# Decode attention and gated MLP on one core: VectorE work moved to ScalarE, one weight chunk loaded by rows, and a small product repeated while TensorE waits

## The chip, the cores and the metric

The kernel runs on one core of a Trainium2 chip. The metric is the device time of one execution in microseconds; lower is better. A separate profiled execution gives the trace.

## The reference

One decode step of a transformer layer in float32, for eight sequences with one new token each. The model width is 1024; there are 32 query heads over 4 key and value heads of size 128, a window of the last 1024 cached positions, and an MLP of width 3584.

```python
x = A_x                                       # (8, 1, 1024)
def attention(x):
    q = (x @ wq).reshape(8, 1, 32, 128)       # wq 1024 x 4096
    k, v = the last 1024 positions of the caches, each shared by 8 query heads
    p = softmax(q @ k.T * 128 ** -0.5)
    return (p @ v).reshape(8, 1, 4096) @ wo   # wo 4096 x 1024
def mlp(x):
    return (gelu(x @ w_gate) * (x @ w_up)) @ w_down   # 1024 x 3584, twice; 3584 x 1024
h = x + attention(layernorm(x))
out = h + mlp(layernorm(h))
```

Every weight and every cache entry is used once for eight tokens, so some 111 MB have to come in from HBM for little arithmetic.

## The kernel before

**Loads.** SyncE (SP) issues all weight loads, in order, into two SBUF buffers `buf[0]` and `buf[1]` of 64 KB a partition (8.4 MB). There are seven passes `k`: the query projection, scores, values, the output projection (`WO`), two for gate and up (`GU0`, `GU1`) and one for the down projection (`DN`). Each has a half `a` on `buf[0]` and a half `b` on `buf[1]`; the last has `a` only. A load waits until TensorE has finished with its buffer. Behind those come the late loads: three parts `wd0` to `wd2` of the last `a` half (steps 0 to 3, 4 to 6 and 7, by `CUTS`), three `singles` `ws0` to `ws2` (one 128-row chunk of the down matrix each, 512 KB, 4 KB a row), and the last chunk in two column blocks `we0` and `we1` (`ends`, 256 KB each). Last come 15 tiny `tag` loads; the k-th longest of them has k rows.

**TensorE** runs one loop over the passes (L457). In each half it first turns a token tile (`turn`, L441: eight 128x128 transposes into the PSUM tile `tt`), then makes `products` (L450): eight steps of four matmuls, which stand abreast in four column groups of 32; each float32 matmul is two records in the trace. Steps 0 to 3 go into the first half of the accumulator `ob[s]`, steps 4 to 7 into the second. TensorE waits at L434 on a counter `go`, which GpSimd raises: GpSimd walks the waits of all passes in TensorE's order (L422 to L429). In pass `WO` there are two more products: `fold` (L469), which brings the attention output into the order of the rows, and `res` (L475), which brings the residual `h_sb` into the output's order in `fin`.

**Between the halves** VectorE and ScalarE turn a finished accumulator into the next tokens: scaling, softmax, the value sum over the eight sequences that share a tile (one instruction each, L302 and L305), GELU times up, and copies from `tt` into the token tiles `st` (L242, L270, L288, L312), into `at` (L377), and `widen` (L351). SP and DMA are not waited for there unless a load is late.

**The end.** `d1` gathers the last accumulator's two halves and `d0` (residual and early parts): L396 after step 3 and L398 after step 7. Then `add` (L485) makes, for each of `ws0` to `ws2`, eight matmuls into `fin`, with eight for `d1` behind the first of them; L496 does the last chunk, column block by column block. ScalarE copies the two blocks out (L402); SP and ScalarE store them.

**Order and waits.** `Flow` adds a semaphore wait in front of an instruction only where that engine hasn't seen that count yet (`missing`, L55). It does not know what another engine's count implies.

Of the kernel before, what the change touches and what calls it, by code (L numbers as in the profile page):

```python
# [8 lines left out]
P = 128  # L9
B = 8  # L10
# [22 lines left out]
SINGLE = 3  # L33
TAGS = 15


class Flow:


    def __init__(self, nc):  # L40
        self.nc = nc
        self.sems = []
        self.done = {}
        self.seen = {}
        self.own = {}
        for name in ("tensor", "vector", "scalar", "gpsimd"):
            self.own[name] = self.sem(name)
            self.done[name] = 0
# [5 lines left out]

    def missing(self, engine, waits):  # L55
# [4 lines left out]
        for s, v in need.values():  # L60
            self.seen[engine, s.name] = v
        return list(need.values())

# [9 lines left out]
    def run(self, engine, make, *waits, mark=True):  # L73
        ins = self.start(engine, make, waits)
        if not mark:
            return None
        self.done[engine] += 1
        ins.then_inc(self.own[engine], 1)
        return self.own[engine], self.done[engine]

    def move(self, name, out, src, *waits, engine="sync"):
        s = self.sem(name)
        self.start(engine, lambda e: e.dma_start(out, src), waits).then_inc(s, 16)
        return s, 16
# [7 lines left out]
def pe_marks():  # L92

    names = ["t"]
    for k in range(PASSES):
        names += [f"a{k}h", f"a{k}"]
        if k < DN:
            names += [f"ta{k}", f"b{k}h", f"b{k}"]
            if k == WO:
                names += ["fold", "res"]  # L100
            names += [f"tb{k}"]
    return names


def pe_waits():

    names = ["t"]
    for k in range(PASSES):
        names += [f"a{k}", f"a{k}m", f"a{k}l"]
        if k < DN:  # L110
            names += [f"ta{k}", f"b{k}", f"b{k}m"]
            if k == WO:
                names += ["fold", "res"]
            names += [f"tb{k}"]
    return names


def decode_block(nc, x, w, dn, single, ends, outs):
# [3 lines left out]
    names = pe_marks()  # L122
# [12 lines left out]
    xs = [sb(f"xs{i}", P, D) for i in range(2)]  # L135
# [28 lines left out]
    for i in range(SINGLE):  # L164
        t = buf[1][:, i * D:(i + 1) * D]
        singles.append((t, move(f"ws{i}", t, single[i], pe(f"b{GU1}"))))
# [9 lines left out]
    for k in range(TAGS, 0, -1):  # L176
# [8 lines left out]
    h_sb = sb("h_sb", P, D)  # L185
    d0 = sb("d0", P, N)
    clear = [run("gpsimd", lambda e, t=t: e.memset(t, 0.0)) for t in (xs[1], xs[0], h_sb, d0)]
# [6 lines left out]
    to_rows = sb("to_rows", P, 2, ROWS)  # L194
    z = run("gpsimd", lambda e: e.memset(to_rows, 0.0))
# [3 lines left out]
        ident[:, 2 * 32:4 * 32].rearrange("p (c m) -> p c m", c=2)[:, :, 0:B]), z)  # L199
# [11 lines left out]
    need = {}  # L211
# [27 lines left out]
    def tokens_in(ready):  # L239

        xt = t8[:, :, 0:ROWS].rearrange("p n (b s) -> p n b s", s=STEP)[:, :, :, 0]
        a = run("vector", lambda e: e.tensor_copy(  # L242
            st[0].rearrange("p (c r b) -> p c r b", c=NC, b=B),
            xt.unsqueeze(2).to_broadcast([P, NC, P // B, B])), *ready)
        b = run("scalar", lambda e: e.copy(st[1], st[0]), a)  # L245
        return a, b

    ready = layernorm(x_sb, xs[1], x_in, "ln1", clear[0])
# [7 lines left out]
    for s, h in enumerate("ab"):  # L256
        need[f"{h}0"] = [*landed[0, s], *st_ok[s], *o_free[s]]
        half = run("scalar", lambda e: e.mul(tq[s], ob[s][:, 0:N], scale), pe(f"{h}0h"))  # L258
        tok = run("vector", lambda e: e.scalar_tensor_tensor(  # L259
            xs[s][:, 0:N], ob[s][:, N:2 * N], scale, tq[s], op0=ALU.mult, op1=ALU.add),  # L260
            pe(f"{h}0"), half, clear[1 - s])
        o_free[s] = (tok,)
        need[f"t{h}0"] = [tok, *tt_free]
        z = run("vector", lambda e: e.memset(st[s], 0.0), pe(f"{h}0"))
        for k0 in range(2):
            for g in range(2):
                dst = view(st[s], k0 * HB * P + g * 2 * 32, (32, 2), (P + REP, HB), (REP // 2, 2), (1, REP // 2))
                src = view(tt, g * 2 * 32, (HB, 2), (1, HB), (32, 2), (P, REP // 2))
                st_ok[s] = tt_free = (
                    run("vector", lambda e: e.tensor_copy(dst, src), pe(f"t{h}0"), z),)  # L270
# [3 lines left out]
    for s, h in enumerate("ab"):  # L274
        need[f"{h}1"] = [*landed[1, s], *st_ok[s], *o_free[s]]
        nmax, tot, rtot, sh = (
            sb(f"{n}{s}", P, k) for n, k in (("nmax", 1), ("tot", 1), ("rtot", 1), ("share", HB))
        )
        tok = run("vector", lambda e: e.tensor_reduce(  # L279
            out=nmax, in_=ob[s], axis=AX.X, op=ALU.max, negate=True), pe(f"{h}1"))  # L280
# [4 lines left out]
        tok = run("vector", lambda e: e.reciprocal(rtot, tot), tok)  # L285
        share.append((sh, run("vector", lambda e: e.tensor_scalar(
            sh, own, rtot, None, op0=ALU.mult), tok, own_ok)))
        a = run("vector", lambda e: e.tensor_copy(st[s][:, 0:N], tt[:, 0:N]), pe(f"t{h}1"))  # L288
        b = run("scalar", lambda e: e.copy(st[s][:, N:2 * N], tt[:, N:2 * N]), pe(f"t{h}1"))
        st_ok[s] = tt_free = (a, b)  # L290


    for s, h in enumerate("ab"):
        need[f"{h}2"] = [*landed[2, s], *st_ok[s], *o_free[s]]
        sh, tok = share[s]
        out = xs[s][:, 0:DH]
        for i in range(2):
            o3 = ob[s][:, i * N:(i + 1) * N].rearrange("p (b d) -> p b d", b=HB)
            ready = pe(f"{h}2" + "h" * (1 - i))
            for b in range(HB):  # L300
                if (i, b) == (0, 0):
                    tok = run("vector", lambda e: e.tensor_scalar(  # L302
                        out, o3[:, b], sh[:, b:b + 1], None, op0=ALU.mult), tok, ready)
                else:
                    tok = run("vector", lambda e: e.scalar_tensor_tensor(  # L305
                        out, o3[:, b], sh[:, b:b + 1], out, op0=ALU.mult, op1=ALU.add), tok, ready)
# [3 lines left out]
        for g in range(2):  # L310
            turned = tt[:, 64 * g:64 * g + 64].rearrange("p (b h) -> p h b", h=REP)
            tok = run("vector", lambda e: e.tensor_copy(  # L312
# [6 lines left out]
    for s, h in enumerate("ab"):  # L319
# [12 lines left out]
        h_sb[0:ROWS], x_sb, fin[0:ROWS]), pe("fold"), clear[2])  # L332
    need["res"] = [h_ok]
    run("scalar", lambda e: e.copy(d0[0:32], fin[0:32, 0:N]), pe("res"), clear[3])  # L334
# [9 lines left out]
    ex = sb("ex", 32, N)  # L344
# [3 lines left out]
    def widen(i0, i1, *ready):  # L348

        src = at[:, EARLY + 2 * i0:EARLY + 2 * i1].rearrange("p (i e) m -> p i (e m)", e=2)  # L350
        return run("vector", lambda e: e.tensor_copy(  # L351
# [3 lines left out]
    for k, nb, q0 in ((GU0, NQ, 0), (GU1, DF // N - NQ, NQ * (N // P))):  # L355
# [10 lines left out]
        if k == GU1:  # L366

            first_ok = widen(0, STEPS // 2, pe(f"a{k}"))
            ex_ok = run("scalar", lambda e: e.copy(d0[96:P], g0[96:P]), g_ok, clear[3])
        a = run("vector", lambda e: e.tensor_mul(u0, ge, ob[1][:, 0:N]), pe(f"b{k}h"), ge_ok)  # L370
        b = run("vector", lambda e: e.tensor_mul(u1, ge, ob[1][:, N:2 * N]), pe(f"b{k}"), ge_ok)  # L371
        o_free[1] = (b,)
        hm_ok = run("vector", lambda e: e.tensor_add(xs[1][:, 0:N], u0, u1), a, b, pe(f"tb{k - 1}"))
        need[f"tb{k}"] = [hm_ok, *tt_free]
        if k == GU0:
            used = (run("vector", lambda e: e.memset(ge[96:P], 1.0), b),)
        at_ok = run("vector", lambda e: e.tensor_copy(  # L377
# [4 lines left out]
        if k == GU0:  # L382
            st_ok = [(run("vector", lambda e, s=s: e.tensor_copy(lent[s], at[:, 0:STEPS]), at_ok),)
                     for s in range(2)]
        else:
            late_ok = widen(STEPS // 2, STEPS, at_ok)
            tok = run("scalar", lambda e: e.copy(ex, xs[1][96:P, 0:N]), hm_ok)
            d0_ok = run("vector", lambda e: e.tensor_add(d0[0:32], d0[0:32], ex), tok, res_ok)
    need[f"a{GU1}m"] = landed[GU1, 0][1:]
# [6 lines left out]
    tok = run("vector", lambda e: e.tensor_add(d1, ob[0][:, 0:N], d0), pe(f"a{DN}h"), d0_ok, ex_ok)  # L396
    fl.done["tensor"] = len(names)
    d1_ok = run("vector", lambda e: e.tensor_add(d1, ob[0][:, N:2 * N], d1), pe(f"a{DN}"), tok)  # L398
# [3 lines left out]
    done = [run("scalar", lambda e: e.copy(o_fin[:, a:b], d_ps), (fl.own["tensor"], len(names) + 1 + i))  # L402
# [19 lines left out]
    for name in pe_waits():  # L422
        left = fl.missing("gpsimd", need.pop(name, []))
# [6 lines left out]
    assert not need, need  # L430
# [12 lines left out]

    def products(s, cuts):
        for i in range(STEPS):
            if i in cuts:
# [117 lines left out]
```

## Time and profile before

| | |
|---|---|
| median of 3 runs | 267.03 us (265.92 to 267.09) |
| the profiled execution | 266.8 us, its span 265.5 us |
| TensorE matmuls, busy | 143.2 us (54%), 1024 records |
| VectorE, busy | 39.9 us (15%), 84 instructions |
| ScalarE, busy | 18.3 us (7%), 27 instructions |
| GpSimd, busy | 5.6 us (2%), 15 instructions |
| mean granted TensorE clock | 0.814 |
| moved by DMA | 111.38 MB, mean 420 GB/s |

A row of the page's fifth part, of the groups by line or of a timeline names the kernel's line, the engine, the operation, the tile written and the tiles read. A window row holds the stretch, its length, the busy microseconds and instruction counts of PE, PEld, DVE, ACT and POOL, the granted TensorE clock, the share of the 16 DMA engines that moved data, and GB/s. "DMA to landing" is the time from the issue of a load to its completion.

### The profile page before, as it was taken

To read this page: it belongs to the slowest core of one execution; us is meant where nothing else is said; L and a number is where in the kernel's file an instruction comes from. 1 tells how busy PE (TensorE), PEld (TensorE's weight loads), DVE (VectorE), ACT (ScalarE), POOL (GpSimd) and SP (SyncE) were. 2 spreads that over 40 slices of the span, in tenths; PEclk is the share of its full clock that TensorE was granted. 3 is DMA by queue.
4 is the path that set the end of the run, shared out by engine and by line. 5 is a ranking of instruction groups with operands and counts; after the bars stand their busy time and mean duration, and the time that the engine had idled before them with its cause. 6 is when DMAs were issued, how large, how long until landed. Compare 5 with 4: busy or idle time off the path is not lost. (4 is left out here: it accounts for less than half of the span.)

```text
span 265.5 us, 2397 instructions
## 1 busy us (share of the span) xinstructions
PE 143.2 (54%) x1024; PEld 49.8 (19%) x1024; DVE 39.9 (15%) x84; ACT 18.3 (7%) x27; POOL 5.6 (2%) x15
## 2 busy tenths in 40 slices
PE   0023914915926716717718609717929557527666
PEld 0021211211221112202212202103313212102223
DVE  0330030030030110410410100251001401102301
ACT  1010000200020010000000000031200001000000
POOL 8000000000000000000000000000000000000000
PEclk9999985885865975975986956985898997977959
DMA  8997999899989998999899999999999999999992
GB/s 318 469 454 346 464 474 444 355 464 474 434 365 464 474 425 375 464 474 415 385 464 474 405 395 464 465 395 415 454 405 405 464 400 464 400 459 411 412 406 85
DMA packets 3716, 111.38 MB, mean 420 GB/s; under 512 B 632, under 2 KB 888, under 8 KB 1536
## 3 DMA queue, kind: packets, MB, share of 16 engines
q1 hardware_dynamic: 3552, 111.23, 97.5%
q10 hardware_dynamic: 160, 0.10, 0.1%
q8 instruction: 2, 0.03, 0.0%
q14 instruction: 2, 0.02, 0.0%
HBM read 111.19 MB, written 0.13 MB: 419 GB/s over the span
## 5 line engine op out<-in xcount | busy, mean ns | idle before, releaser
L450 PE MATMUL o<-w,st 128*32 128x512 f32 x832 | 121.5, 746 | 83.7 <-PEq L434 83.7
L450 PEld LDWEIGHTS o<-w,st 128*32 128x32 f32 x832 | 33.7, 133 | 163.0 <-issue 163.0
L441 PE MATMUL tt<-ident,xs 128*128 128x128 f32 x104 | 16.6, 311 | 33.6 <-PEq L434 33.6
L441 PEld LDWEIGHTS tt<-ident,xs 128*128 128x128 f32 x104 | 13.3, 160 | 44.2 <-issue 44.2
L327 DVE TENSOR_TENSOR y_sb<-o,y_sb 128x512 f32<-128x512 f32 x3 | 2.1, 691 | 32.7 <-PE o L450 32.7
L279 DVE TENSOR_REDUCE nmax<-o 128x1 f32<-128x1024 f32 x2 | 2.5, 1225 | 30.1 <-PE o L450 30.1
L259 DVE SCALAR_TENSOR_TENSOR xs<-o,tq 128x512 f32<-128x512 f32 x2 | 1.4, 691 | 32.5 <-PE o L450 32.5
L305 DVE SCALAR_TENSOR_TENSOR xs<-o,share,xs 128x128 f32<-128x128 f32 x14 | 4.9, 350 | 4.3 <-PE o L450 3.8
L281 ACT ACTIVATE xs<-o,nmax 128x1024 f32<-128x1024 f32 x2 | 2.2, 1114 | 37.0 <-DVE nmax L279 37.0
L362 DVE TENSOR_TENSOR g<-o,g 128x512 f32<-128x512 f32 x2 | 1.4, 692 | 22.4 <-PE o L450 22.4
L302 DVE TENSOR_SCALAR xs<-o,share 128x128 f32<-128x128 f32 x2 | 0.7, 351 | 24.4 <-PE o L450 24.4
L325 ACT COPY y_sb<-o 128x512 f32<-128x512 f32 x1 | 0.6, 586 | 50.3 <-PE o L450 50.3
L370 DVE TENSOR_TENSOR u<-ge,o 128x512 f32<-128x512 f32 x2 | 1.4, 688 | 17.6 <-PE o L450 17.6
L371 DVE TENSOR_TENSOR u<-ge,o 128x512 f32<-128x512 f32 x2 | 1.4, 687 | 14.3 <-PE o L450 14.3
L258 ACT ACTIVATE tq<-o 128x512 f32<-128x512 f32 x2 | 1.2, 597 | 30.0 <-PE o L450 30.0
L242 DVE COPY st<-tt 128x1024 f32<-128x1024 f32 x2 | 2.4, 1224 | 4.3 <-PE tt L441 4.3
L361 ACT COPY g<-o 128x512 f32<-128x512 f32 x2 | 1.2, 586 | 26.6 <-PE o L450 26.6
L312 DVE COPY st<-tt 128x512 f32<-128x512 f32 x4 | 2.6, 685 | 2.6 <-PE tt L441 2.6
L245 ACT COPY st<-st 128x1024 f32<-128x1024 f32 x2 | 2.1, 1044 | 10.2 <-DVE st L242 10.2
L226 ACT ACT_TABLE_LOAD x2 | 2.6, 1283 | 2.9 <-POOL ident L182 2.9
L219 DVE BATCH_NORM_STATS2 ln_bn<-x_sb 64x6 f32<-64x512 f32 x2 | 1.3, 677 | 8.3 <-DMA x_sb<-x 8.3
L334 ACT COPY d<-fin 32x512 f32<-32x512 f32 x1 | 0.6, 575 | 28.3 <-PE fin L475 28.3
(59 smaller groups left out, 41.2 us busy)
## 6 DMA issues: line engine op xcount, KB each, us to landing
w<-ends SPq DMA_DIRECT2D x5, 4096.0 KB, 23.6
w<-ends SPq DMA_DIRECT2D x1, 3072.0 KB, 30.5
w<-ends SPq DMA_DIRECT2D x3, 512.0 KB, 15.2
w<-ends SPq DMA_DIRECT2D x1, 1024.0 KB, 32.6
w<-ends SPq DMA_DIRECT2D x2, 256.0 KB, 16.2
w<-w SPq DMA_DIRECT2D x10, 29.2
out<-o_fin SPq DMA_DIRECT2D x1, 64.0 KB, 1.6
out<-o_fin ACTq DMA_DIRECT2D x1, 64.0 KB, 1.7
```

Of the source, the lines that this page charges most:

```text
L226: tok = run("scalar", lambda e: e.activation(sd, ve, AF.Sqrt), tok)
L242: a = run("vector", lambda e: e.tensor_copy(st[0].rearrange("p (c r b) -> p c r b", c=NC, b=B), xt.unsqueeze(2).to_broadcast([P, NC, P // ...
L245: b = run("scalar", lambda e: e.copy(st[1], st[0]), a)
L259: tok = run("vector", lambda e: e.scalar_tensor_tensor(xs[s][:, 0:N], ob[s][:, N:2 * N], scale, tq[s], op0=ALU.mult, op1=ALU.add), pe(f"{h ...
L279: tok = run("vector", lambda e: e.tensor_reduce(out=nmax, in_=ob[s], axis=AX.X, op=ALU.max, negate=True), pe(f"{h}1"))
L281: tok = run("scalar", lambda e: e.activation(xs[s], ob[s], AF.Exp, bias=nmax, accum_out=tot), tok)
L305: tok = run("vector", lambda e: e.scalar_tensor_tensor(out, o3[:, b], sh[:, b:b + 1], out, op0=ALU.mult, op1=ALU.add), tok, ready)
L312: tok = run("vector", lambda e: e.tensor_copy(heads[:, g], turned.unsqueeze(2).to_broadcast([P, REP, P // 2 // B, B])), pe(f"t{h}2"))
L327: tok = run("vector", lambda e: e.tensor_add(y_sb, part, y_sb), ready, tok)
L362: g_ok = run("vector", lambda e: e.tensor_add(g0, ob[0][:, N:2 * N], g0), pe(f"a{k}"), tok)
L441: ins = nc.tensor.transpose(t8[:, i, :], src[:, i * P:(i + 1) * P], ident)
L450: ins = nc.tensor.matmul(ob[s][32 * r:32 * r + 32, c:c + N], st[s][:, i * P + 32 * r:i * P + 32 * r + 32], buf[s][:, (i * NQ + r) * N:(i * ...
```

## The change

1. **VectorE to ScalarE.** The copies out of `tt` (token tiles, score tiles, turned heads, `at`, `lent`, `widen`) become ScalarE copies. The value sum's eight instructions a half become two multiplications over a whole half accumulator and one reduction. Gate times up is summed before it is multiplied. `d0` gets the early part of the down product as a further block of rows instead of an addition. By count 40 VectorE instructions fewer.
2. **GpSimd.** Five memsets of five tiles become one over a tile `zeros` that holds them all.
3. **Waits.** `Flow` keeps with every completion what its engine had waited for (`told`, `implied`), and leaves out a wait that another wait implies. The two lists of TensorE's marks and waits become one list `pe_order`.
4. **`ws0` by rows.** The first single chunk is loaded by three loads, of rows 0 to 31, 32 to 119 (88 rows, by 11 DMA engines) and 120 to 127. Its product leaves `add`: two matmuls of 512 columns, behind step 7, add it into the second half of the last accumulator, so that L398 waits for them.
5. **The repeated product.** TensorE repeats the first matmul of `res` in three gaps: twice in front of step 0 and twice in front of step 4 of the last pass, and four times in front of step 4 of the `b` half of `GU1`. The result lies in `fin` and is overwritten when `ws1` starts its group there.

```diff
+ROWCUTS = (0, 32, 120, P)
+AGAIN = (((0, DN, 2), (STEPS // 2, DN, 2)), ((STEPS // 2, GU1, 4),))
...
+        if i == 0:
+            here = fl.sem("ws0")
+            for a, b in zip(ROWCUTS, ROWCUTS[1:]):
+                fl.start("sync", lambda e: e.dma_start(t[a:b], single[i][a:b]), [pe(f"b{GU1}")]).then_inc(
+                    here, 16)
...
-    clear = [run("gpsimd", lambda e, t=t: e.memset(t, 0.0)) for t in (xs[1], xs[0], h_sb, d0)]
+    clear = run("gpsimd", lambda e: e.memset(zeros, 0.0))
...
-        a = run("vector", lambda e: e.tensor_copy(
+        a = run("scalar", lambda e: e.copy(
             st[0].rearrange("p (c r b) -> p c r b", c=NC, b=B),
...
-            for b in range(HB):
-                if (i, b) == (0, 0):
-                    tok = run("vector", lambda e: e.tensor_scalar(
-                        out, o3[:, b], sh[:, b:b + 1], None, op0=ALU.mult), tok, ready)
-                else:
-                    tok = run("vector", lambda e: e.scalar_tensor_tensor(
-                        out, o3[:, b], sh[:, b:b + 1], out, op0=ALU.mult, op1=ALU.add), tok, ready)
+            tok = run("vector", lambda e: e.scalar_tensor_tensor(
+                av[:, i], o3, rtot, own.unsqueeze(2).to_broadcast([P, HB, DH]),
+                op0=ALU.mult, op1=ALU.mult), tok, own_ok, pe(f"{h}2" + "h" * (1 - i)))
+        tok = run("vector", lambda e: e.tensor_reduce(
+            out=out, in_=av.rearrange("p i b d -> p d (i b)"), axis=AX.X, op=ALU.add), tok)
...
-            d0_ok = run("vector", lambda e: e.tensor_add(d0[0:32], d0[0:32], ex), tok, res_ok)
+            d0_ok = run("scalar", lambda e: e.copy(d0[32:64], xs[1][96:P, 0:N]), hm_ok)
...
-    d1_ok = run("vector", lambda e: e.tensor_add(d1, ob[0][:, N:2 * N], d1), pe(f"a{DN}"), tok)
+    odd_done = fl.own["tensor"], len(names) + 1
+    d1_ok = run("vector", lambda e: e.tensor_add(d1, ob[0][:, N:2 * N], d1), odd_done, tok)
...
+    def repeat_residual(n):
+        with nc.Fori(0, n, engines=[mybir.EngineType.PE]):
+            nc.tensor.matmul(
+                fin[0:32, 0:N], spread.rearrange("p r b -> p (r b)"), h_sb[:, 0:N],
+                start=True, stop=True)
...
     def products(s, cuts):
         for i in range(STEPS):
+            for at_step, k, n in AGAIN[s]:
+                if i == at_step:
+                    with nc.tensor.If(it == k):
+                        repeat_residual(n)
             if i in cuts:
                 wait()
...
-    for i, (t, here) in enumerate(singles):
-        add(lambda j: at[:, LAST - SINGLE + i, :], lambda j: t[:, j * QW:(j + 1) * QW], here,
-            *([res_ok, at_ok] if i == 0 else []), start=(i == 0))
+    (t, here), *rest = singles
+    for ch in range(2):
+        tok = run("tensor", lambda e: e.matmul(
+            ob[0][64 * ch:64 * ch + 32, N:2 * N], at[:, LAST - SINGLE, :], t[:, ch * N:(ch + 1) * N],
+            start=False, stop=True, skip_group_check=True), here, at_ok, mark=(ch == 1))
+    for i, (t, here) in enumerate(rest):
+        add(lambda j: at[:, LAST - SINGLE + 1 + i, :], lambda j: t[:, j * QW:(j + 1) * QW], here,
+            start=(i == 0))
```

More of the change, by code (lines that the diff above doesn't have):

```diff
@@ L121, in decode_block, with before_mark @@
     scale = DH ** -0.5
-    names = pe_marks()
+    order = pe_order()
+    names = [n for kind, n in order if kind == "mark"]
+    need = {}
+    def before_mark(v):
+        out, left = [], v
+        for kind, n in order:
+            if kind == "wait":
+                out += need.get(n, [])
+            else:
+                left -= 1
+                if left == 0:
+                    break
+        return out
+    fl.before_mark = before_mark
     def pe(name):
```

130 lines of the change are left out of this document (69 added, 61 removed).

## The prediction

> **What bounds the kernel now.** I read the page's slices and queues first, then the chain that ended last, then the last 40 us by timeline, loads and narrow windows.
>
> ```profile
> span 265.5 us, 2397 instructions
> ...
> PE 143.2 (54%) x1024; PEld 49.8 (19%) x1024; DVE 39.9 (15%) x84; ACT 18.3 (7%) x27; POOL 5.6 (2%) x15
> ...
> PEclk9999985885865975975986956985898997977959
> DMA  8997999899989998999899999999999999999992
> ...
> q1 hardware_dynamic: 3552, 111.23, 97.5%
> q8 instruction: 2, 0.03, 0.0%
> q14 instruction: 2, 0.02, 0.0%
> ...
> w<-w SPq DMA_DIRECT2D x10, 29.2
> ```
>
> The loads fill the 16 DMA engines for 97.5% of the span; only the last slice is empty. A whole buffer takes 29.2 us from issue to landing, while its 8.4 MB of the 111.23 MB are worth about 19.5 us of the engines (8.4/111.23 of 97.5% of 265.5). So each load is issued some 9.7 us before its turn: what happens between the loads may become microseconds longer without an engine running dry. What can be won lies at the end.
>
> ```profile
> 254.25 6.39 PE o L450 x32
> ...
> 260.73 0.69 DVE d L398
> ...
> 261.48 1.52 PE fin L485 x48
> 263.00 0.26 PE fin L496 x8
> ...
> 263.28 0.48 ACT o_fin L402 x2
> ```
>
> That is the chain: steps 4 to 7 of the last pass, the second sum into d1, 64 small products (two records for each of 32 matmuls), the copies. Beside it stand the loads (first the three of the last pass, wd0 to wd2, then the three single chunks ws0 to ws2, then the end blocks we0 and we1), and how many DMA engines still work:
>
> ```profile
> L83 SPq DMA_DIRECT2D w<-ends x3: 327/432/433, 223.2 to 224.0; - x3
> DMA to landing us min/median/max: 23.6/30.5/32.6
> L83 SPq DMA_DIRECT2D w<-ends x3: 327/432/434, 243.6 to 244.4; - x3
> DMA to landing us min/median/max: 14.3/15.2/16.0
> L83 SPq DMA_DIRECT2D w<-ends x2: 431/434/437, 244.9 to 245.4; - x2
> DMA to landing us min/median/max: 16.1/16.2/16.3
> ```
> ```profile
> 259.60:259.80 0.20, 0.20 (x5) 0.00 (x0) 0.00 (x0) 0.00 (x0) 0.00 (x0) 0.61 0.74 187
> 260.00:260.40 0.40, 0.40 (x8) 0.12 (x4) 0.00 (x0) 0.00 (x0) 0.00 (x0) 1.00 0.23 79
> 260.40:261.00 0.60, 0.60 (x20) 0.35 (x12) 0.27 (x1) 0.00 (x0) 0.00 (x0) 1.00 0.15 50
> 261.00:261.20 0.20, 0.04 (x4) 0.00 (x0) 0.20 (x1) 0.00 (x0) 0.00 (x0) 1.00 0.13 26
> ```
>
> Issue plus time to landing: wd1 lands at about 254.1 (223.6 + 30.5; PE begins step 4 right behind it), wd2 at 256.6, the single chunks at 257.9, 259.1 and 260.4, the end blocks at 261.0 and 261.7. The last column but one, the DMA share, times 16: 11.8 engines work at 259.7, 3.7 at 260.2, 2.4 at 260.7 and two until 261.2. So most engines are through by about 260.0, and two or three end up to 1.2 us later; every load waits for its slowest engine. The landing is told 0.45 us behind the last engine (261.7 against 261.2). But PE is later still:
>
> ```profile
> 237.21 6.33 PE L450 MATMUL o<-w,st 128*32 128x512 f32 x32 [6.08 <-PEq L434]
> 246.93 3.64 PE L450 MATMUL o<-w,st 128*32 128x512 f32 x32 [0.65 <-PEq L434]
> 254.25 6.34 PE L450 MATMUL o<-w,st 128*32 128x512 f32 x32 [3.69 <-PEq L434]
> 262.81 0.62 PE L496 MATMUL fin<-w,at 128*32 128x128 f32 x16
> ```
>
> The same 32 records take 3.64 us in the pass's first half and 6.34 in its second, and the last product ends at 263.43 (262.81 + 0.62), 1.75 us behind the last landing. Two things can be gained: those 2.7 us of PE, and behind them the late DMA engines.
>
> **The product repeated in the gaps.** Each repeat is one matmul, two records that follow each other; what it writes is overwritten later. The rows for price and clock:
>
> ```profile
> 173.36 1.05 PE L475 MATMUL fin<-h_sb,spread 128*32 128x512 f32 x4 [1.52 <-PEq L434]
> ```
> ```profile
> L457 PEldq COMPARE_BRANCH  x8: 76/209/224, 1.5 to 257.2; - x8
> ```
> ```profile
> 92.50:95.91 3.41, 1.06 (x8) 0.86 (x8) 1.08 (x3) 1.60 (x3) 0.00 (x0) 1.00 0.80 346
> 130.04:133.46 3.42, 1.65 (x16) 0.86 (x8) 1.40 (x4) 0.00 (x0) 0.00 (x0) 1.00 1.20 517
> 249.50:252.93 3.43, 1.07 (x12) 0.16 (x4) 0.69 (x1) 0.00 (x0) 0.00 (x0) 1.00 0.91 387
> 252.93:259.75 6.82, 5.50 (x28) 1.59 (x32) 0.00 (x0) 0.00 (x0) 0.00 (x0) 0.50 1.00 395
> ```
>
> The stretches are cut where the granted clock changes. Behind 1.06 and 1.07 us of PE work in 3.4 us it fell to 0.50; behind 1.65 us it held. In L475 two matmuls ran in two column groups at once, so its 1.05 us are two records in a row and their drain, 0.2 by the first half's form (32 records, four abreast, in 3.64: 0.43 a row); a repeat is 0.86 us. In the last pass's gap, 250.57 to 254.25, two repeats make 1.7 us, with 0.2 for a branch each some 2.1, so they end at 252.7, ahead of wd1: they cost nothing, and of any 3.4 us at least 1.4 to 1.7 hold work (3.41 less the 1.6 to 2.0 left idle). That is nearest to the 1.65 that held. I take the clock as held; the other end is a fall as now.
>
> [...]
>
> In the pass before, four repeats (3.4 us and branches) stand in a gap of 6.1 us; if the clock holds there, its last half ends 2.7 us earlier, at 240.9, which only brings the issue of the single chunks forward: their turn on the engines comes 10 us later anyway. The two repeats ahead of the last pass end near 245.4 or, with that half at the old speed, near 248.4. In the second case the first half starts 1.5 us late and still ends before wd1.
>
> **The end on PE.** Steps 4 to 7 start at 254.25 and take 3.64: 257.89 (wd2, 256.6, is there for step 7). ws0's product now follows as two wide matmuls into the accumulator, the form of L475: 1.05, to 258.94. Then the second sum: 0.09 us of start (now from 260.64 to 260.73) and 0.69, to 259.72. Behind it stood 64 records from 261.48 to 263.43, 1.95 us; now 48 (ws0's 16 are gone, ws1's are done while VectorE adds, so in truth 48 is the add, ws2 and the blocks): 1.46 and 0.06 of start (261.42 to 261.48) give 261.24.
>
> **ws0 by rows.** A row costs 0.16 us on an engine ((260.4 - 257.9)/2 for eight rows). Now every engine has eight. Then: 32 rows give each 2; 88 rows give engines 0 to 10 eight each; 8 rows one each to engines 0 to 7. So engines 0 to 7 get 3 more (+0.48 us), 8 to 10 get 2 more (+0.32), 11 to 15 six fewer (-0.96). No row shows an 88-row load; the ends are all 88 rows on one engine (+13 us) and a spread even over 16 (0). The edit's own words say 11, and I take that.
>
> [...]
>
> Which engines are late? Three fetches of instructions fall among the loads:
>
> ```profile
> q8 instruction: 1, 0.02, 6.4%
> ```
> ```profile
> q14 instruction: 1, 0.01, 1.0%
> ```
> ```profile
> q14 instruction: 1, 0.01, 1.9%
> ```
>
> These are from 5.0 to 5.9, 169 to 171 and 251 to 252 us (6.4% of 16 engines in 0.9 us is one engine for 0.92 us; the others 0.3). Three fetches, and up to three late engines at the end. The tag loads of k rows put a packet on each of engines 0 to k-1; by the count of such packets behind each engine's last block, the last to end is engine 11, then 3, then 2. Engine 11 is relieved; 3 and 2 are loaded. The first fetch comes before any edited work and stays. The two of q14 bring code of engines that no view names. VectorE loses 40 instructions of its 84 and the waits between them, GpSimd four; ScalarE goes from 27 to some 50, below VectorE's count of now. If they were VectorE's and GpSimd's, they need not come any more, and I hold this likelier than that they stay.
>
> Then the bulk ends at 260.0 + 0.48, engine 11 at 261.2 - 0.96: the last landing is 260.5 + 0.45 = 260.9, and 0.3 us for the last eight records and their drain make 261.2. PE's own chain said 261.24. Both ends meet there, 2.2 us before 263.43. What comes behind PE (copies, stores) stays: 263.43 to 265.5.
>
> **Moved to ScalarE.**
>
> ```profile
> L279 DVE TENSOR_REDUCE nmax<-o 128x1 f32<-128x1024 f32 x2 | 2.5, 1225 | 30.1 <-PE o L450 30.1
> ...
> L289 ACT COPY st<-tt 128x512 f32<-128x512 f32 x2 | 1.2, 586 | 3.4 <-PE tt L441 3.4
> L245 ACT COPY st<-st 128x1024 f32<-128x1024 f32 x2 | 2.1, 1044 | 10.2 <-DVE st L242 10.2
> L305 DVE SCALAR_TENSOR_TENSOR xs<-o,share,xs 128x128 f32<-128x128 f32 x14 | 4.9, 350 | 4.3 <-PE o L450 3.8
> ```
>
> The value sum took four of 0.35 us behind the last product; now one of 0.69 and a reduction of 1.2: +0.5 us. The copy of a whole turned tile on ScalarE is 1.04 where two halves ran side by side: +0.4. Both lie under the 9.7 us of queued loads: nothing. Without that cover they would add up to about 5 us over the passes. The final pass's widening and copies end before 249, five microseconds ahead of their use. SP issues two loads more (0.45 each) ahead of the other chunks and the tags: under the same backlog.
>
> **Sum.** 266.8 for the profiled execution (its span and 1.3 us around it) less 2.2 is 264.6; the median of the runs, 267.03, is 0.2 higher, so 264.8 us.
>
> **Rivals.** (1) The late fetches stay: engine 3, late until about 261.05, gets 0.48 more: 261.53 + 0.45 + 0.3 = 262.3 instead of 263.43, so 1.1 less: 265.9. That is 0.4% and counts as no change, since 0.5% (1.3 us) is about what a measurement of this kernel can tell. Were only engine 2's fetch left, it would be 265.3. For this rival: no view says whose code it is. (2) The clock falls all the same: steps 4 to 7 end at 260.64 as now, ws0's 1.05 us is added in front of the sum and 0.49 saved behind it (1.95 less 1.46): 267.6, no change. (3) Slower: the repeats are in PE's own order. If the clock stays low from 237 on, two repeats (3.8 us) and a turn some 1 us longer stand in front of the last pass, which now follows the turn within 0.65 us: it starts near 251 instead of 246.9, its first half takes up to 6.3 us, to 257.3, and with two repeats (2.1) and 3.64 more step 7 ends at 263.0, 5.1 us behind my 257.9: 270.0. It decides from step 4 being 3.5 us late (2.2 + 1.3). Against it: the PEclk slices of 6.6 us show 7 from 239 and 9 from 246 us on, so the clock is back by the end of those 6.33 us of work. (4) The 88 rows are left to one engine: 80 rows more, 12.8 us, lie on it behind wd2, and ws0 and all behind it land that much later, near 277. For it, no row of such a load; against it, the edit's words.
>
> **Chances.** The forecast, with 265.3 as its neighbour: faster, 0.68. (1) 0.15 and (2) 0.06: no change, 0.21. (3) 0.08 and (4) 0.03: slower, 0.11. The range begins at 263.9: the last landing is followed by 0.3 us of PE at the least and comes at the earliest when the bulk of the engines ends now, 260.0 + 0.45, which is 0.45 us less than the forecast's 260.9, and the runs spread by as much. It reaches to 266.9, which takes in (1) and the highest spread of the runs shown (265.92 to 267.09); (2) to (4) stay out.
>
> **What would show it.** Right: granted clock 1.0 from 246 to the end, the last 32 records of L450 in about 3.6 us, the two-matmul product right behind them, last PE work near 261.3, DMA share under one engine after 260.6, no q14 row after 0. Wrong: clock 0.5 behind 254; two engines at work until 261.5 (rival 1); PE starting step 4 after 254.3; PE queues stalled at the loops.

## The result, and the profile after

The changed kernel takes 268.01 us (median of 10 runs, 267.57 to 269.47); the kernel before takes 265.95 on the same chip (10 runs, 265.62 to 267.09). The ratio is 1.0076, with a 95% interval of 1.0057 to 1.0096: slower by 0.8%, where 264.8 us and faster was forecast. One thing is needed to read the numbers that follow: executions of the kernel before lie in two groups, here eight near 265.9 us and two near 267.1, and the profile on which the prediction was made (266.8 us) is of the upper one.

The page of the changed kernel, profiled at 267.8 us: span, busy engines, the granted clock and the DMA share by slices, and the new reduction.

```profile
span 266.2 us, 2425 instructions
PE 145.5 (55%) x1028; PEld 50.3 (19%) x1028; DVE 28.6 (11%) x47; ACT 28.5 (11%) x49; POOL 5.3 (2%) x11
PEclk9999995975975956966965968975977999799979
DMA  8997999799979997999799979997999999999994
...
L334 DVE TENSOR_REDUCE zeros<-av 128x128 f32<-128x1024 f32 x2 | 3.7, 1871 | 0.1
```

VectorE is busy for 28.6 us, from 39.9, and ScalarE for 28.5, from 18.3. In the last slice of the DMA row stands a 4 where a 2 stood: the loads go on for longer. The chain of waits, in order of time (start, length, what), and the matmuls of the last pass by timeline say the same:

```profile
243.35 19.61 DMA w<-ends
...
263.01 0.47 PE fin L541 x8
```
```profile
250.30 1.88 PE L475 MATMUL fin<-zeros,spread 128*32 128x512 f32 x4
254.16 5.54 PE L489 MATMUL o<-w,st 128*32 128x512 f32 x32 [1.98 <-PEq L462]
259.49 1.06 PE L530 MATMUL o<-w,at 128*32 128x512 f32 x4
...
263.01 0.43 PE L541 MATMUL fin<-w,at 128*32 128x128 f32 x8 [0.30 <-DMA w<-ends]
```

The last block lands at 262.96 (243.35 + 19.61), 1.3 us behind the 261.7 of before, and now the last product waits for it. Two repeats stand in the gap (four records), yet steps 4 to 7 take 5.54 us. Windows of the changed kernel (stretch, length, busy time of five engines, granted clock, DMA share, GB/s) show both; under them one window of the kernel before:

```profile
251.08:254.49 3.41, 1.43 (x7) 0.30 (x9) 0.25 (x1) 0.00 (x0) 0.00 (x0) 1.00 0.89 372
254.49:257.90 3.41, 3.41 (x20) 1.08 (x16) 0.00 (x0) 0.00 (x0) 0.00 (x0) 0.50 1.05 213
255.00:258.00 3.00, 3.00 (x17) 0.81 (x12) 0.00 (x0) 0.00 (x0) 0.00 (x0) 0.52 1.02 194
261.00:262.00 1.00, 0.59 (x24) 0.59 (x27) 0.35 (x1) 0.00 (x0) 0.00 (x0) 1.00 0.80 304
262.00:262.40 0.40, 0.40 (x24) 0.37 (x16) 0.06 (x1) 0.00 (x0) 0.00 (x0) 1.00 0.75 156
```
```profile
255.00:258.00 3.00, 3.00 (x20) 0.91 (x16) 0.00 (x0) 0.00 (x0) 0.00 (x0) 0.50 1.02 410
```

From 255 to 258 us every DMA engine is busy in both kernels, but the changed one moves 194 GB/s where 410 went. The missing 216 GB/s over 3 us are 0.65 MB, which at 410 GB/s is 1.6 us of all engines. Twelve of the 16 (0.75) still work at 262.2, where before 3.7 worked at 260.2, 2.4 at 260.7 and none at 262.2. The packets in that stretch, of the changed kernel and then of the kernel before:

```profile
DMA packets 164, 0.58 MB, mean 194 GB/s; under 512 B 25, under 2 KB 25, under 8 KB 161
...
q1 hardware_dynamic: 164, 0.58, 102.4%
```
```profile
DMA packets 328, 1.23 MB, mean 410 GB/s; under 512 B 33, under 2 KB 33, under 8 KB 323
...
q1 hardware_dynamic: 328, 1.23, 102.3%
```

Nearly all data packets here are rows of 4 KB. 102.4% of 16 engines for 3 us are 49.2 us; by the 139 packets of 512 bytes and more that is 0.35 us a row. Before: 49.1 us by 295, 0.17. The stretch is that of `ws0`, of the last rows of `wd2` ahead of it and, before, of `ws1` behind it. So rows of the chunk loaded in three parts cost about twice as much.

The fetches of instructions left the loads, as forecast: no instruction row stands between 150 and 260 us. They are not gone, though, as the prediction's sign had it ("no q14 row after 0"); they come behind the loads, from 262 us on:

```profile
q14 instruction: 2, 0.02, 2.0%
q8 instruction: 1, 0.02, 1.4%
```

Behind the last product there are 2.8 us to the span's end, and 1.6 from the span to the time of the run (267.8 - 266.2); in a profile of before from the lower group, below, it is 2.2 and 1.3. With the 1.3 us of the later landing that makes 2.2 us, the distance of those two profiles (267.8 and 265.6). The two stores and these late fetches fall together there; that the one delays the other was not tested.

### The profile page after: what moved, and what is told of

It reads as the page before. It is cut to its first block, busy times and chain, and to the rows that moved or that the text cites. A ratio compares the mean times of both kernels' runs of the same rounds, so it can differ in the third digit from the quotient of the medians.

```text
span 266.2 us, 2425 instructions
## 1 busy us (share of the span) xinstructions
PE 145.5 (55%) x1028; PEld 50.3 (19%) x1028; DVE 28.6 (11%) x47; ACT 28.5 (11%) x49; POOL 5.3 (2%) x11
## 5 line engine op out<-in xcount | busy, mean ns | idle before, releaser
L489 PE MATMUL o<-w,st 128*32 128x512 f32 x832 | 116.3, 717 | 79.0 <-PEq L462 47.4
L469 PE MATMUL tt<-ident,zeros 128*128 128x128 f32 x104 | 16.5, 311 | 35.8 <-PEq L462 35.8
L469 PEld LDWEIGHTS tt<-ident,zeros 128*128 128x128 f32 x104 | 13.3, 159 | 46.2 <-issue 46.2
L475 PE MATMUL fin<-zeros,spread 128*32 128x512 f32 x16 | 7.4, 594 | 0.0
L331 DVE SCALAR_TENSOR_TENSOR av<-o,rtot,own 128x512 f32<-128x512 f32 x4 | 3.0, 750 | 31.3 <-PE o L489 31.3
L341 ACT COPY st<-tt 128x512 f32<-128x512 f32 x4 | 2.1, 588 | 35.4 <-PE tt L469 35.4
L316 ACT ACTIVATE zeros<-o,nmax 128x1024 f32<-128x1024 f32 x2 | 2.2, 1114 | 33.6 <-DVE nmax L314 33.6
L334 DVE TENSOR_REDUCE zeros<-av 128x128 f32<-128x1024 f32 x2 | 3.7, 1871 | 0.1
L398 ACT COPY u<-o 128x512 f32<-128x512 f32 x2 | 1.2, 586 | 21.0 <-PE o L489 21.0
L227 POOL MEMSET zeros<- 128x3712 f32 x1 | 3.2, 3191 | 0.0
L279 ACT COPY st<-tt 128x1024 f32<-128x1024 f32 x2 | 2.0, 1012 | 7.7 <-PE tt L469 7.7
```

What stands on the lines that cost most here:

```text
L227: clear = run("gpsimd", lambda e: e.memset(zeros, 0.0))
L279: a = run("scalar", lambda e: e.copy(st[0].rearrange("p (c r b) -> p c r b", c=NC, b=B), xt.unsqueeze(2).to_broadcast([P, NC, P // B, B])) ...
L316: tok = run("scalar", lambda e: e.activation(xs[s], ob[s], AF.Exp, bias=nmax, accum_out=tot), tok)
L331: tok = run("vector", lambda e: e.scalar_tensor_tensor(av[:, i], o3, rtot, own.unsqueeze(2).to_broadcast([P, HB, DH]), op0=ALU.mult, op1=A ...
L334: tok = run("vector", lambda e: e.tensor_reduce(out=out, in_=av.rearrange("p i b d -> p d (i b)"), axis=AX.X, op=ALU.add), tok)
L341: tok = run("scalar", lambda e: e.copy(heads[:, g], turned.unsqueeze(2).to_broadcast([P, REP, P // 2 // B, B])), pe(f"t{h}2"))
```

## The experiments

Theory A, called ports in the expectations: a row costs more when the rows of a load lie in neighbouring partitions and are fewer than 128. Rivals: every further load, or any load of fewer than 128 rows, costs something by itself; the source in HBM is at fault; the repeats hold up TensorE; the lost clock sets the end. Edits are against the changed kernel unless said otherwise, and ratios against runs of the kernel before on the same chip.

### The chunk in one load

```diff
-ROWCUTS = (0, 32, 120, P)
+ROWCUTS = (0, P)
```

> The changed kernel with ws0 as one load of 128 rows again, all else as changed. [...] Theory load (three more rows on engines 0 to 7 at 0.16 us each are what came late): at most 0.5 us under the changed kernel. Theory repeats (the loops on TensorE cost the time): no change from the changed kernel, 1.007.

Measured: 266.34 us, ratio 1.0003 (0.9984 to 1.0022). The windows:

```profile
251.20:254.62 3.42, 1.43 (x7) 0.30 (x9) 0.33 (x1) 0.00 (x0) 0.00 (x0) 1.00 0.90 375
254.62:258.04 3.42, 3.42 (x20) 1.09 (x16) 0.00 (x0) 0.00 (x0) 0.00 (x0) 0.50 1.03 413
```

The rate of before is back, and so is the time. The loss lies in the three loads; the rest of the change costs nothing that the interval would show. The clock still falls, behind 1.43 us of work in 3.42, so the two repeats do not hold it here, with or without the loads by rows.

### No repeats

```diff
-AGAIN = (((0, DN, 2), (STEPS // 2, DN, 2)), ((STEPS // 2, GU1, 4),))
+AGAIN = ((), ())
```

> The changed kernel without the repeated products. Ports: the DMA rate falls in 254 to 259 us as in the changed kernel, the last landing stays near 263.0 and, since TensorE at half clock for all of steps 4 to 7 is later still by about 1 us, the time is 0 to 1.5 us above the changed kernel's: 1.007 to 1.013 of before. Theory repeats: 1 to 2 us under the changed kernel's, about 1.0 of before.

Measured: 268.8 us, ratio 1.0106 (1.0076 to 1.0136), the interval overlapping that of the change. By timeline:

```profile
254.15 5.34 PE L489 MATMUL o<-w,st 128*32 128x512 f32 x32 [3.68 <-PEq L462]
261.27 1.05 PE L530 MATMUL o<-w,at 128*32 128x512 f32 x4 [1.78 <-DMA w<-ends]
```

Steps 4 to 7 begin when they did with the repeats (254.16), so the repeats hold up nothing. The expectation had half the clock for all of these steps; they took 5.34 us against 5.54 with the repeats, so the two repeats did not help the clock here either. Without them TensorE is through with step 7 at 259.49 and waits 1.78 us for `ws0`. In this one profile `ws0` and the last block landed later than in the changed kernel, the block by 1.7 us; why was not settled.

### Four loads of 32 rows, and eight of 16

```diff
-ROWCUTS = (0, 32, 120, P)
+ROWCUTS = (0, 32, 64, 96, P)                  # quarters
+ROWCUTS = (0, 16, 32, 48, 64, 80, 96, 112, P) # eighths
```

> The changed kernel with ws0 in four loads of 32 rows, each on 16 engines, so that every engine has its eight rows again and only the place of the rows differs. [...] Load: the engines' work is equal, so the time is one_load's, within 0.3 us.

> The changed kernel with ws0 in eight loads of 16 rows, each on 16 engines. [...] A fixed cost for each further load instead (as between one_load and quarters, a third of their distance for each of three): eight loads lie 7/3 of that distance behind one_load, with rows no slower. Load: as one_load.

Measured: quarters 268.31 us, ratio 1.0086 (1.0057 to 1.0115); eighths 267.74, 1.0066 (1.0042 to 1.0089). From 255 to 258 us, quarters and then eighths:

```profile
DMA packets 207, 0.65 MB, mean 216 GB/s; under 512 B 53, under 2 KB 53, under 8 KB 203
...
q1 hardware_dynamic: 207, 0.65, 101.0%
```
```profile
DMA packets 244, 0.61 MB, mean 204 GB/s; under 512 B 98, under 2 KB 98, under 8 KB 241
...
q1 hardware_dynamic: 244, 0.61, 104.4%
```

A data row takes 0.31 us (48.5 by 154) and 0.34 (50.1 by 146). No view names the engine of a row, but in the groups of loads by themselves, below, a load of 32 rows and one of 16 leave 16 packets under 512 B each (64 by four, 128 by eight), as one of 128 does. If every engine at work on a load leaves one, an estimate from these counts, the shares are eight rows an engine as in one load, and uneven shares are not needed for the loss: also with equal shares a row costs twice as much. Twice as many loads did not cost more, so the price is not one of each load. It also speaks against a strict form of theory A, by which a row costs the more the fewer neighbours its load holds: by themselves eight loads of 16 cost 1.6 times as much as four of 32 (1.97 against 1.22 us a row, below), in the queue 1.1 times (0.34 against 0.31). Why the two differ was not shown.

### One load, and three repeats in the last gap

```diff
-ROWCUTS = (0, 32, 120, P)
+ROWCUTS = (0, P)
-AGAIN = (((0, DN, 2), (STEPS // 2, DN, 2)), ...
+AGAIN = (((0, DN, 2), (STEPS // 2, DN, 3)), ...
```

> ws0 as one load, and three repeats instead of two in the last gap. The clock fell in one_load at 254.6 behind 3.4 us with 1.4 us of TensorE work; with a third repeat (0.86 us) that stretch holds 2.3 us. Theory clock: 1.0 granted up to the end, steps 4 to 7 in 3.65 instead of 5.34 us, last product at the last landing (261.8) plus 0.35 instead of 262.9; the time is 0.7 to 0.9 us under one_load, 0.997 of before. Theory of the landing alone (the late engine 11 sets the end): no change against one_load, within 0.2 us.

Measured: 265.84 us (265.49 to 266.05), ratio 0.9992 (0.9976 to 1.0007). Windows, cut in steps of 3.41 us from the last change of the granted clock in this profile, and timeline (in the profiles of the kernel before and of the changed kernel all changes of the clock lie whole multiples of 3.41 us apart, 3.41 to 23.9):

```profile
250.47:253.88 3.41, 2.57 (x9) 0.44 (x4) 0.69 (x1) 0.00 (x0) 0.00 (x0) 1.00 0.90 377
253.88:257.29 3.41, 3.12 (x32) 1.07 (x32) 0.00 (x0) 0.00 (x0) 0.00 (x0) 1.00 0.99 399
```
```profile
254.17 3.64 PE L489 MATMUL o<-w,st 128*32 128x512 f32 x32 [1.12 <-PEq L462]
257.90 1.05 PE L530 MATMUL o<-w,at 128*32 128x512 f32 x4
...
261.71 0.42 PE L541 MATMUL fin<-w,at 128*32 128x128 f32 x8 [0.25 <-DMA w<-ends]
```

Behind 2.57 us of work the clock held. The steps took the 3.64 and 1.05 us of the prediction, and TensorE then waited for the last block, landing at 261.7 as before. The 2.7 us that TensorE saves end in that wait: no run of 12 is above 266.05 (6 of 23 of the kernel before are above 266.5), but the median is the same.

### One load, no repeats

Both edits: `ROWCUTS = (0, P)` and `AGAIN = ((), ())`.

> ws0 as one load and no repeats: what is left is the instructions moved to ScalarE, the shorter waits, and ws0's product in front of the second sum. Clock theory: 0.50 from about 253 to 260, steps 4 to 7 in 6.3 us, ws0's product behind them, the last product near 263.6; 0.7 us above one_load, 1.002 to 1.004 of before. If the repeats did nothing: as one_load.

Measured: 266.7 us (265.72 to 267.67), ratio 1.0028 (1.0008 to 1.0047). The profiled execution was its shortest, 265.72, and had the full clock without repeats, where 0.50 was expected:

```profile
254.29 3.64 PE L489 MATMUL o<-w,st 128*32 128x512 f32 x32 [3.65 <-PEq L462]
```
```profile
249.18:252.59 3.41, 1.46 (x16) 0.28 (x8) 0.69 (x1) 0.00 (x0) 0.00 (x0) 1.00 0.97 413
252.59:256.00 3.41, 1.71 (x16) 0.65 (x20) 0.00 (x0) 0.00 (x0) 0.00 (x0) 1.00 1.00 411
```

The stretches are again cut in steps of 3.41 us from this profile's last change of the clock. The gap lies across two of them, so that each holds enough work: 1.46 us and more. In other profiles the cuts lie otherwise against steps 4 to 7 (a cut at 249.18 and the steps from 254.29 here, 250.47 and 254.17 with one load and three repeats, 251.08 and 254.16 in the changed kernel). An execution in which one whole window falls into the gap would lose the clock; that would spread the runs over 2 us as seen, but no profile of a long one was taken.

### Sixteen-row loads from alternate halves

```diff
-ROWCUTS = (0, 32, 120, P)
+ROWCUTS = tuple((a, a + 16) for i in range(0, 64, 16) for a in (i, 64 + i))
...
-            for a, b in zip(ROWCUTS, ROWCUTS[1:]):
+            for a, b in ROWCUTS:
```

> The eight loads of 16 rows in another order: rows 0, 64, 16, 80, 32, 96, 48, 112 and the 15 behind each, everything else as in eighths. [...] Theory source (neighbouring rows of 4 KB read by 16 engines at once are slow in HBM), or a cost for each load: as eighths, within 0.3 us.

Measured: 267.5 us, ratio 1.0057 (1.0034 to 1.008). From 255 to 258 us:

```profile
DMA packets 289, 0.78 MB, mean 261 GB/s; under 512 B 102, under 2 KB 102, under 8 KB 285
...
q1 hardware_dynamic: 289, 0.78, 103.3%
```

A row takes 0.27 us (49.6 by 187) against 0.34: only the order of the eight loads changed. So it counts, too, which loads are next to each other in the queue. That is in the direction of theory A, which speaks of the rows of one load, but part of the loss alone comes back, and the times by themselves do not tell it from its rivals.

### Other rows of the source, the same places in SBUF

```diff
-ROWCUTS = (0, 32, 120, P)
+ROWCUTS = (0, 32, 64, 96, P)
...
-    e.dma_start(t[a:b], single[i][a:b])
+    e.dma_start(t[a:b], single[i].rearrange("(r j) d -> j r d", j=4)[a // 32])
...
+    parts[-SINGLE] = parts[-SINGLE].reshape(4, 32, D).transpose(1, 0, 2).reshape(P, D)
```

> Quarters with the chunk's rows stored in another order in HBM, so that each load of 32 rows reads every fourth row of the 512 KB, while the rows in SBUF stay where they were. Theory ports: as quarters, mean 4 KB packet near 300 ns, 1.008 of before. Theory source: as one_load, 162 ns and 1.000.

Measured: 268.24 us, ratio 1.0085 (1.0061 to 1.0109), as the quarters with neighbouring source rows (1.0086). From 255 to 258 us:

```profile
255.00:258.00 3.00, 2.54 (x24) 0.62 (x16) 0.00 (x0) 0.00 (x0) 0.00 (x0) 1.00 1.01 224
```

The rate stays low. Which rows of HBM a load reads makes no difference; that rival falls.

### Groups of loads by themselves

The kernel before, with twelve groups of loads in front, each waited for before the next; rows of 16 KB, 2 MB a group where all 128 rows are loaded:

```diff
+    patterns = [
+        [(0, P, 1)],
+        [(0, 64, 1), (64, P, 1)],
+        [(a, a + 32, 1) for a in range(0, P, 32)],
+        [(a, a + 16, 1) for a in range(0, P, 16)],
+        [(a, P, 4) for a in range(4)],
...
+    for i, loads_ in enumerate(patterns):
+        here = fl.sem(f"probe{i}")
+        for a, b, step in loads_:
+            nc.sync.dma_start(buf[1][a:b:step, 0:4096], w[1][a:b:step, 0:4096]).then_inc(here, 16)
+        nc.sync.wait_ge(here, 16 * len(loads_))
```

> The kernel before, with twelve groups of loads put in front of all others, one group behind the other, each waited for: 16 KB rows of the same 2 MB into a buffer that is filled afresh later. The groups, by partitions: one load of 128; two of 64; four of 32; eight of 16; four of 32 that take every fourth partition; 32, 88 and 8 as in the change; eight of 8 that take every fourth partition of a half (engines 0 to 7 alone, 64 rows); eight of 8 neighbours (64 rows); four of 8 with every fourth partition, begun at 16 (32 rows); 120 and 8; 88 alone; 128 again. One load of 128 at 27 GB/s an engine takes 4.9 us and about 2 us around it. [...] Theory of the short load (any load of fewer than 128 rows is slow for itself): all but the first and last at half rate, the spread ones too. If none is slow here, the cost in the kernel comes from meeting other loads.

Measured, in one run (406.85 us in all). The windows of six groups: two loads of 64 neighbours; four of 32; eight of 16; four of 32 rows, every fourth partition; 32, 88 and 8 rows; one of all 128. The last two columns are the DMA share and GB/s; each window goes from the issue to the landing.

```profile
9.50:22.00 12.50, 1.94 (x8) 1.57 (x8) 2.82 (x7) 1.25 (x2) 0.00 (x0) 1.00 0.78 168
22.00:34.20 12.20, 0.00 (x0) 0.00 (x0) 0.00 (x0) 0.00 (x0) 0.00 (x0) 1.00 0.80 172
34.20:52.70 18.50, 0.00 (x0) 0.00 (x0) 0.00 (x0) 0.00 (x0) 0.00 (x0) 1.00 0.85 113
52.70:61.30 8.60, 0.00 (x0) 0.00 (x0) 0.00 (x0) 0.00 (x0) 0.00 (x0) 1.00 0.69 244
61.30:77.40 16.10, 0.00 (x0) 0.00 (x0) 0.00 (x0) 0.00 (x0) 0.00 (x0) 1.00 0.60 130
133.80:140.90 7.10, 0.00 (x0) 0.00 (x0) 0.00 (x0) 0.00 (x0) 0.00 (x0) 1.00 0.77 295
```

The DMA share times 16 times the window over 128 rows gives, from the top, 1.22, 1.22, 1.97, 0.74, 1.21 and 0.68 us a row. So 64 or 32 neighbours at a time cost 1.8 times, 16 neighbours 2.9 times as much as one load, and 32 rows a load, taken from every fourth partition, 1.1 times. The change's own cut costs 1.8 times. Two more groups, one load of 120 rows with one of 8, and one load of 88 rows alone:

```profile
108.60:122.20 13.60, 0.00 (x0) 0.00 (x0) 0.00 (x0) 0.00 (x0) 0.00 (x0) 1.00 0.71 154
122.20:133.80 11.60, 0.00 (x0) 0.00 (x0) 0.00 (x0) 0.00 (x0) 0.00 (x0) 1.00 0.55 124
```

They give 1.21 and 1.16 us a row (over 128 and 88 rows), so 88 or 120 neighbours are as dear as 32. Loads of eight rows cost 0.73 us a row at every fourth partition of 32 (64 rows in all), 0.80 in a smaller group of these (32 rows), and 1.70 as neighbours, so a short load is not slow for being short. The group left over, one load of 128 at the very start, gives 0.72 beside other loads.

One load of 128 landed 7.1 us behind its issue, where 4.9 and about 2 were expected. The price is one of neighbours, but it does not grow evenly as they get fewer: 64 and 32 cost the same (1.22 us a row), 16 more (1.97), and 88 and 120 about as much as 32 (1.16 and 1.21). By what path a load reaches SBUF no view shows, so the cause behind these prices was not shown.

The groups also tell over how many engines a load goes, as an estimate from the packets under 512 B: 16 for one load of 128, 16 a load in the groups of 64, 32 and 16 rows, 11 for 88 rows, 23 for 120 and 8 together, 8 a load in the groups of eight rows. In the kernel it is the same: the changed one has 19 more of them than the one before (651 and 632), which is 16, 11 and 8 for its three loads less 16 for the one. With one such packet an engine, the 88 rows go over 11 engines, as the edit had it.

### The four loads of 32, every fourth partition

```diff
-ROWCUTS = (0, 32, 120, P)
+ROWCUTS = (0, 1, 2, 3, 4)
...
-    e.dma_start(t[a:b], single[i][a:b])
+    e.dma_start(t[a:P:4], single[i][a:P:4])
```

> Quarters again, with the same number of loads, rows and bytes for each engine, but each load takes every fourth partition (and the row that belongs to it) instead of 32 neighbours. In the row of loads measured by themselves, neighbours moved at half rate (a 16 KB row in 1211 ns) and every fourth partition at full rate (741 ns). Theory ports: 4 KB packets near 165 to 190 ns, most engines through near 260.0 and the late one near 261.3, the time of one_load, 266.3 (1.000 to 1.002 of before). Theory of the number of loads, or of splitting as such: as quarters, 268.3 (1.0085).

Measured: 265.85 us, ratio 1.0003 (0.9984 to 1.0022), against 1.0086 for the quarters of neighbours. From 255 to 258 us:

```profile
DMA packets 371, 1.24 MB, mean 412 GB/s; under 512 B 72, under 2 KB 72, under 8 KB 368
...
q1 hardware_dynamic: 371, 1.24, 103.1%
```

49.5 us by 299 rows is 0.17 again. As many loads, as many rows in each and, by the 64 packets under 512 B in either group of four above, as many engines; only which partitions a load holds differs (and with them the source rows, which made no difference above), and the loss is gone. This settles that the price is in which partitions of SBUF a load holds: 0.31 us a row for 32 neighbours, 0.17 for every fourth. By what mechanism neighbours cost more, no view shows.

### The kernel before once more, and with the repeats alone

The first is the kernel before, unchanged. The second is the kernel before with the function of the repeats, a wait that keeps the repeats from overwriting the residual too early, and these counts:

```diff
+AGAIN = (((0, DN, 2), (STEPS // 2, DN, 3)), ((STEPS // 2, GU1, 4),))
```

> The kernel before once more, for a second profile of it. Its runs fall into two groups, near 265.8 and near 267.0, and the profile I predicted from (266.8) belongs to the upper one. Theory clock: a run of the lower group shows clock 1.0 in steps 4 to 7, 3.65 us for them, and the last product right behind the last landing near 261.7. Rival: the lower group has the earlier last landing and the same clock.

> The kernel before with the repeated products alone (two, three in the last gap, four in the pass before). Theory clock: it removes the upper group of the runs, so that all lie within 265.4 to 266.2; median 265.7, ratio 0.997 to 1.0 by the mean. Rival, that the repeats cost TensorE time or bring a further instruction fetch: 266.3 or more.

Measured: 265.63 us in the one run of the first; 265.5 (265.34 to 266.09) for the second, ratio 0.9988 (0.9976 to 1.0). The first by windows and timeline:

```profile
250.13:253.54 3.41, 2.01 (x20) 0.41 (x12) 0.69 (x1) 0.00 (x0) 0.00 (x0) 1.00 0.94 396
253.54:256.95 3.41, 2.68 (x28) 1.01 (x32) 0.00 (x0) 0.00 (x0) 0.00 (x0) 1.00 1.02 413
```
```profile
254.27 3.64 PE L450 MATMUL o<-w,st 128*32 128x512 f32 x32 [2.12 <-PEq L434]
...
261.72 0.43 PE L496 MATMUL fin<-w,at 128*32 128x128 f32 x8 [0.21 <-DMA w<-ends]
```

Here, too, the gap (2.12 us, since the first half ran slowly, 5.19 us from 246.95, and ended late) lies across two windows, and the clock held. This execution has what the prediction meant to win: the last 32 records in 3.64 us, and the last product waiting for the last block at 261.7. The step from 266.8 to 265.6 was there before any change. The repeats alone, three of them in the last gap, keep the clock in the profile of the second:

```profile
254.26 3.64 PE L461 MATMUL o<-w,st 128*32 128x512 f32 x32 [1.14 <-PEq L435]
```

They have the lowest ratio that was run, though not one clear of the others: they take away the upper group (12 runs within 0.75 us), and gain 0.1%, in an interval that just reaches no change.

## Why the prediction was wrong

**`ws0` by rows: the step that failed.** The number of rows on each engine was taken as the cost, at 0.16 us a row, with the ends "all 88 rows on one engine" and "even over 16". The 0.16 came from loads of all 128 partitions, the only kind in that part of the trace; in the loads by rows it measured 0.35. Instead of 0.48 us later for the bulk and a last landing at 260.9, twelve engines worked at 262.2 and the last block landed at 262.96, 2.1 us behind the forecast. (That the medians lie 2.06 us apart is another sum: 1.3 us of later landing and 0.9 behind the last product.) The bounds should have been on the price of a row as well as on the count. The count itself fits the packets under 512 B (16, 11 and 8 for the three loads). But that engines 0 to 7 get three rows more and 11 to 15 six fewer, the +0.48 and -0.96 us of the forecast, no run shows, since no view names the engine of a row; what the runs show in its place is 0.35 us a row, by itself 1.8 times the price of one load, and twelve engines at work at 262.2. The prediction weighed a number of engines and no price by partitions. Rival 4 looked at the same loads, but for another reason: one engine with 88 rows.

**The clock and the end on PE: the right size, from the wrong base.** The steps take 3.64 and 1.05 us when the clock holds, as worked out. But the 1.75 us between the last landing and TensorE's end belonged to one profiled execution of the upper group, and the forecast took its 2.2 us off 267.03, where ten runs have a median of 265.95: 1.1 us of the gain was there already. In the profile of the lower group the landing sets the end. Over the profiles with the full DMA rate the times part in the same way: 266.55 to 266.8 us in the three where the clock fell behind the last gap (before, the chunk in one load, every fourth partition), 265.44 to 265.72 in the four where it held. The shortest of the three runs shown, 265.92 against 267.03 and 267.09, could have warned of this. And the clock, taken as held, fell: "nearest to the 1.65 that held" was not good enough, as 1.43 us of work were in the stretch, in the change and in the chunk in one load. That lies within the 1.4 to 1.7 of the prediction (3.41 less 1.6 is 1.8, not 1.7), so the amount was right and what it would do was not. Three repeats held in both profiles taken with them, where the gap had room for them. In the change itself the last product waited for the landing, by 0.30 us, so the lost clock did not set its end, but stood close behind. Rival 2, the fall, came true, but with the time set by the loads; that 268.01 lies near its 267.6 is chance.

**The late engines: right, and worth nothing here.** The fetches of q14 at 170 and 251 us no longer came among the loads, as forecast. With the chunk in one load fewer engines are late for it:

```profile
260.00:260.40 0.40, 0.40 (x7) 0.12 (x5) 0.00 (x0) 0.00 (x0) 0.00 (x0) 1.00 0.09 27
260.40:261.00 0.60, 0.60 (x14) 0.33 (x10) 0.33 (x1) 0.00 (x0) 0.00 (x0) 1.00 0.06 24
```

That is 1.4 and one engine, where 3.7 and 2.4 worked before. But the last landing stayed at 261.7 (the run with three repeats), since one or two late engines are enough (1.9 at 260.7 there). So the forecast's second half, that engine 11 ends earlier by six rows, is what had to bring the gain. Whether it could with uneven loads spread over the partitions was not tried.

**The moves to ScalarE and the repeats' place: right.** The reduction takes 1.87 us, not 1.2, and the rest fits; with one load and three repeats the changed kernel (0.9992) and the old one with the repeats alone (0.9988) are alike, so the moves cost and bring nothing that shows. The repeats delayed nothing (254.16 with, 254.15 without), which rules out rival 3.

## What to carry to other kernels

When a load is cut into parts, price a row from a load with the same set of partitions, not from a full one; where none is in the trace, bound the price of a row and not only the number of rows. If a load of 128 rows has to be cut, let each part take every fourth partition: four such parts cost no more here, while neighbours, from 8 to 120 of them in a load, cost 1.7 to 2.9 times as much by themselves. Before a wait is costed from one profile, see to which of the runs' times that profile belongs: a gain read from a long execution may already be in the short ones. A clock held by repeated work needs a margin over the least amount that held once: two repeats made 1.43 us and it fell, three 2.57 and it held.

## What the hardware showed that was not expected

- The DMA engines can all be busy (share 1.02) at half the rate: 194 against 410 GB/s, with rows of the same size. The share says that engines are occupied, not that data flows.
- Four loads of 32 rows cost as one load of 128 when each takes every fourth partition (0.17 us a row in the queue), and twice as much when each takes neighbours (0.31).
- With stretches cut on each profile's own grid of 3.41 us, the clock fell behind 1.43 us of work (the changed kernel, and the chunk in one load) and held behind 1.46 (one load, no repeats), 2.01 (the kernel before, again) and 2.57. In the kernel before and in the changed kernel, over all stretches cut this way, it fell behind none with more than 1.43 and held behind none with less than 1.54 (before, from 225.62). But with other rows of the source it fell near 260.48 (0.57 granted from 260.4 to 261.0, 0.50 from 261.0) behind 1.54 (from 257.07: steps 4 to 6 to 257.54, step 7 from 259.07 to 260.14), more than the 1.46 behind which it held. So these runs show no sharp limit; it lies near 1.5 us, with a blur of 0.08 at the least, and the same gap falls or holds by where the grid lies.
